# Top-k attention and SoLU layer: in the first batch, one query chunk of each pair of heads per step

## The chip, the cores and the metric

One core of a Trainium2 chip. The metric is the device time of one execution in microseconds. The engines are named as in the profile: PE is TensorE, DVE is VectorE, ACT is ScalarE, POOL is GpSimd, SP is the engine whose queue issues all DMAs here.

## The reference

Attention with eight batches, eight heads, 576 tokens and a head size of 64, in which each query keeps only its 32 largest scores, and behind it a SoLU layer over all 4608 tokens (512 to 1024 to 512).

```python
scores = scale * np.matmul(q, k.transpose(0, 1, 3, 2))
kth = np.partition(scores, -top_k, axis=-1)[..., -top_k:-top_k + 1]
scores = np.where(scores >= kth, scores, -1000000000.0)
attn = np.exp(scores - np.max(scores, axis=-1, keepdims=True))
attn = attn / (np.sum(attn, axis=-1, keepdims=True) + 1e-09)
x = np.matmul(attn, v)          # then (B,H,S,D) -> (B*S, H*D)
...
h = x @ w_in
solu = h * softmax(h)
ln = (solu - mean(solu)) / np.sqrt(var(solu) + 1e-06) * g_ln
out = ln @ w_out
```

## The kernel before

The work is done by `fast_path`; `general_path` stands behind a test at the end, and runs only if a check of the results fails.

**Tiling.** Two heads form a pair (four pairs `hp` in a batch), and the first 512 tokens of a batch form four chunks `t` of 128 queries (every fourth token). The last 64 tokens of the two heads of a pair make one more tile, the tail. A *step* handles four chunks and one tail, that is nine tiles `j` of 128 queries by 576 keys: two heads of each of four chunks and the tail of the pair of chunk 1. A batch takes four steps (0 to 3 for the first), and there are 32. The list `steps` says which pair and which `t` each of the four chunks has. Before the change a step is two pairs with two `t` each: steps 0 and 1 hold `t` = 0 and 1 of all pairs, steps 2 and 3 hold `t` = 2 and 3.

**What one step does.** `load_q` fetches its queries, `prep_q` transposes them on PE. `spread` multiplies them by the moments of the keys, and `spread_v`, `spread_r`, `first_p` and `first` make from this a first guess of the threshold. `scores` computes 128x576 scores into PSUM, `evac` (ACT) copies them to SBUF. `count0`, `count1` and `count2` count the scores above the threshold, on DVE or ACT, and `second`, `third`, `side` move it. `nearest` and `best` take the eight scores nearest to it, `kth` picks the 32nd largest, `exps` (ACT) and `keep` (DVE) make the masked exponentials, `inverse` and `norm` (POOL) divide. `transpose_p` and `transpose_last` turn the result on PE, `copy_p`, `copy_pt` and `copy_last` bring it back (ACT), and `attn_v` multiplies it by the values in two parts of two chunks each. `copy_v` writes the result into `xTm`, which holds two tiles of 128 tokens for all heads.

In `attn_v` and `copy_v`, `runs_of` says whether the two chunks of a part are of one pair. If so, one run of matmuls covers both (256 columns, 320 with the tail); if not, each has its own run (128 columns, or 192 with the tail), with other values.

**Keys.** Before a step may start, the keys of its pairs must be there: `load_k` (with the tails qt and kt), `prep_t`, `prep_k` and `moments` on PE, `prep_tc`, `prep_kc` and `moments_c` on ACT. `load_v` fetches the values.

**SoLU.** A tile of 128 tokens needs all four pairs: `mm1` (two halves), `hexp`, `solu`, `square`, `ln`, `transpose_ln`, `copy_ln`, `mm2` (two halves), `store`. The tails of two batches make one tile. Before the change the tiles 0 and 1 of a batch are complete after its second step.

**Weights.** They arrive as 64-bit floats in 16 chunks, which are turned into 32-bit ones on the way: `load_w`, `w_bits` (DVE), `w_low` (ACT), `w_mul` and `w_add` (POOL), for the second matrix `w_gain`. At the end `w_again`, `w_exp` and `w_check` read them once more and test the exponents.

**What sets the order.** Each piece is entered in a list with a time by `at`; the list is sorted by these times, and each engine gets its instructions in that order. The times order the work and are not waited for. A step's times are `i * STEP` plus an entry of a table: `early_times` has one for each of the first four steps, `step_times` is for all others. `key_times` has one column of times for the first batch and one for all others, `first_times` is for the SoLU tiles of the first batch, `last_times` for those after the last step, `weights_times` for the weights. DMAs of SP are not bound to the written order. What two engines exchange is held by semaphores.

**Buffers.** PSUM has two buffers each for scores, spread and `mm1` (`ps_big`), for transposes (`ps_tp`), and for `attn_v`, `mm2` and the moments (`ps_o`). km has two buffers in SBUF, qt, kt and qm one, kT, mom and the values four. The buffer `e` of the weights' low words is also that of `hexp`.

Of the kernel before, what the change touches and what calls it, by code (L numbers as in the profile page):

```python
# [443 lines left out]
def fast_path(  # L444
# [33 lines left out]
    NP = H // 2  # L478
# [34 lines left out]
    steps = []  # L513
    for b in range(B):
        for t in range(NM):
            two = (t % 2 * 2 + t // 2, t % 2 * 2 + 1 - t // 2)
            steps.append((b, [(hp, t // 2 * 2 + n) for hp in two for n in range(2)]))
# [677 lines left out]
    def at(time, f, *args):  # L1195
        todo.append((time, len(todo), f, args))
# [11 lines left out]
        (scores, range(5), [-7.74, -5.46, -3.54, 0.79, 4.68]),  # L1208
# [28 lines left out]
            (load_q, [()], [-136.1]),  # L1237
            (prep_q, [()], [-49.08]),
            (prep_qc, [()], [-46.09]),
            (spread, [()], [-22.56]),  # L1240
            (spread_v, [()], [-13.82]),
            (spread_r, [()], [-12.57]),
            (first_p, [()], [-11.71]),
            (first, [()], [-3.81]),
            (scores, range(5), [-21.73, -13.84, -9.25, -5.8, 5.01]),
            (evac, range(9), [-18.63, -17.61, -9.77, -3.84, -3.2, -0.35, 5.05, 5.55, 8.61]),
            (count0, range(9), [1.43, -2.43, -1.53, -1.4, 2.24, 3.27, 7.16, 8.56, 8.7]),
            (count1, range(9), [19.93, 27.62, 15.8, 24.5, 16.48, 14.52, 25.06, 25.75, 22.05]),
            (count2, range(9), [45.91, 37.67, 35.49, 32.86, 34.21, 33.88, 48.07, 37.74, 40.71]),
            (second, [()], [10.83]),  # L1250
            (third, [()], [28.34]),
            (exps, range(5), [57.94, 49.7, 61.64, 46.09, 40.28]),
            (side, range(3), [46.05, 39.08, 50.36]),
            (inverse, range(3), [64.9, 68.93, 66.47]),
            (count_off, [()], [59.35]),
            (kth, [()], [60.91]),
            (nearest, range(9), [47.42, 50.7, 47.04, 39.24, 40.26, 39.26, 60.08, 59.88, 52.51]),
            (best, range(9), [48.01, 59.72, 47.48, 39.95, 43.29, 42.83, 60.16, 60.15, 59.98]),
            (keep, range(9), [64.38, 62.62, 62.48, 66.91, 67.31, 68.45, 64.67, 62.84, 61.06]),
            (norm, range(9), [78.27, 66.62, 66.94, 72.53, 69.31, 74.77, 76.06, 70.77, 84.71]),  # L1260
            (transpose_p, range(9), [
                78.29, 66.83, 69.62, 80.13, 73.72, 75.25, 77.68, 81.99, 84.88,
            ]),
            (copy_p, range(8), [84.06, 73.04, 72.36, 85.61, 74.57, 77.94, 84.7, 88.91]),
            (copy_pt, [()], [89.53]),
            (transpose_last, range(2), [85.88, 86.4]),
            (copy_last, range(2), [90.93, 96.41]),
            (attn_v, range(2), [91.57, 101.11]),
            (copy_v, range(2), [101.5, 121.24]),
        ],  # L1270
        [
            (load_q, [()], [-63.22]),
            (prep_q, [()], [-26.27]),
            (prep_qc, [()], [-25.87]),
            (spread, [()], [-22.59]),
            (spread_v, [()], [-21.61]),
            (spread_r, [()], [-20.83]),
            (first_p, [()], [-11.31]),
            (first, [()], [-9.51]),
            (scores, range(5), [-23.24, -22.22, -7.58, -5.59, 4.98]),  # L1280
            (evac, range(9), [-20.42, -15.03, -8.31, -7.32, -2.53, -3.83, 4.56, 6.06, 7.69]),
            (count0, range(9), [1.51, -1.93, -5.39, -3.17, 7.48, 1.22, 4.65, 7.36, 7.75]),
            (count1, range(9), [12.6, 21.87, 22.86, 24.54, 22.25, 19.32, 24.46, 22.34, 14.2]),
            (count2, range(9), [36.07, 31.22, 33.95, 29.01, 30.63, 28.45, 27.23, 37.22, 40.08]),
            (second, [()], [9.1]),
            (third, [()], [25.73]),
            (exps, range(5), [54.75, 52.35, 55.64, 60.46, 56.71]),
            (side, range(3), [41.53, 34.61, 56.64]),
            (inverse, range(3), [63.82, 63.6, 73.38]),
            (count_off, [()], [50.44]),  # L1290
            (kth, [()], [60.1]),
            (nearest, range(9), [42.17, 44.33, 56.1, 41.95, 39.38, 37.61, 59.31, 59.5, 58.57]),
            (best, range(9), [43.9, 46.54, 58.59, 43.63, 40.7, 39.89, 59.58, 59.9, 59.07]),
            (keep, range(9), [63.5, 60.13, 60.62, 63.16, 63.01, 60.7, 67.68, 64.74, 65.7]),
            (norm, range(9), [66.68, 64.54, 68.09, 65.27, 68.2, 66.01, 79.57, 78.32, 75.89]),
            (transpose_p, range(9), [66.85, 70.12, 70.62, 71.87, 76.84, 74.5, 81.76, 80.5, 78]),
            (copy_p, range(8), [70.39, 72.11, 74.48, 76.8, 79.63, 77.7, 82.11, 81.19]),
            (copy_pt, [()], [80.01]),
            (transpose_last, range(2), [86.05, 81.84]),
            (copy_last, range(2), [86.37, 83.08]),  # L1300
            (attn_v, range(2), [86.46, 96.54]),
            (copy_v, range(2), [92.8, 98.93]),
        ],
        [
            (load_q, [()], [-76.41]),
            (prep_q, [()], [-32.91]),
            (prep_qc, [()], [-25.84]),
            (spread, [()], [-18.69]),
            (spread_v, [()], [-11.8]),
            (spread_r, [()], [-11.68]),  # L1310
            (first_p, [()], [-10.43]),
            (first, [()], [-9.45]),
            (scores, range(5), [-22.71, -12.67, -7.53, -2.95, 1.7]),
            (evac, range(9), [-12.31, -12.22, -6.84, -6.24, -4.12, -3.99, -1.57, -0.04, 6.99]),
            (count0, range(9), [-2.44, -0.84, 0.69, 19.56, 4.9, 17.24, 7.58, 2.3, 9.88]),
            (count1, range(9), [23.76, 25.39, 28.42, 21.7, 27.47, 25.78, 27.06, 28.55, 25.68]),
            (count2, range(9), [30.97, 37.36, 39.06, 31.65, 36.22, 33.28, 36.55, 49.83, 41.98]),
            (second, [()], [19.61]),
            (third, [()], [28.64]),
            (exps, range(5), [58.03, 56.1, 60.41, 52.39, 48.63]),  # L1320
            (side, range(3), [46.98, 36.8, 49.89]),
            (inverse, range(3), [66.91, 73.37, 74.37]),
            (count_off, [()], [56.97]),
            (kth, [()], [62.82]),
            (nearest, range(9), [49.3, 59.4, 51.74, 39.5, 41.96, 45.32, 60.81, 60.84, 56.14]),
            (best, range(9), [51.85, 60.58, 59.01, 41.93, 45.25, 46.41, 62.37, 62.67, 59.73]),
            (keep, range(9), [63.28, 63.18, 64.23, 72.39, 65.68, 68.64, 70.02, 73.4, 73.34]),
            (norm, range(9), [67.15, 67.42, 68.98, 73.84, 77.05, 75.85, 74.93, 79.44, 78.1]),
            (transpose_p, range(9), [67.2, 74.04, 79.09, 74.96, 78.87, 77.74, 80.44, 83.19, 83.7]),
            (copy_p, range(8), [73.28, 76.39, 80.9, 77.89, 80.14, 79.48, 84.79, 87.36]),  # L1330
            (copy_pt, [()], [87.38]),
            (transpose_last, range(2), [85.91, 87.61]),
            (copy_last, range(2), [88.63, 90.09]),
            (attn_v, range(2), [90.16, 103.01]),
            (copy_v, range(2), [98.48, 115.16]),
        ],
        [
            (load_q, [()], [-66.4]),
            (prep_q, [()], [-35.36]),
            (prep_qc, [()], [-30.84]),  # L1340
            (spread, [()], [-16.76]),
            (spread_v, [()], [-13.17]),
            (spread_r, [()], [-7.35]),
            (first_p, [()], [-6.37]),
            (first, [()], [-2.89]),
            (scores, range(5), [-14.48, -8.24, -4.39, -2.81, -0.97]),
            (evac, range(9), [-9.51, -8.86, -5.93, -6.05, -1.91, -1.98, -0.4, 0.23, 3.86]),
            (count0, range(9), [-1.72, -1.54, 2.05, 6.45, 5.49, 1.09, 2.45, 8.26, 5.24]),
            (count1, range(9), [11.24, 22.02, 18.49, 13.46, 24.31, 11.77, 18.79, 23.05, 15.93]),
            (count2, range(9), [31.11, 28.29, 30.53, 25.47, 34.71, 38.96, 31.66, 44.39, 26.25]),  # L1350
            (second, [()], [9.95]),
            (third, [()], [24.77]),
            (exps, range(5), [60.62, 50.55, 56.29, 53.12, 56.37]),
# [164 lines left out]
    for b in range(B):  # L1518
        rows = out[b * S : b * S + SM, :].rearrange("(p t) m -> p t m", t=NM)
        n = NP * b + 2  # L1520
# [91 lines left out]
```

## Time and profile before

| | us |
|---|---|
| time, median of 3 runs (1288.27 to 1289.8) | 1289.05 |
| span of the profiled execution | 1288.0 |
| PE busy | 1201.0 |
| DVE busy | 1138.5 |
| ACT busy | 1131.1 |
| POOL busy | 479.7 |

Busy time is that of instructions in execution; the end of a matmul is modelled. In the slices of the page a digit is the busy share of a fortieth of the span (32.2 us) in tenths. Three engines are over 85% busy, so the shares alone don't tell which sets the time: the stretches and the waits must be read. The mean clock that PE was granted over the span is 0.966 of full speed.

### The profile page before, as it was taken

How to read it: one execution, taken by the hardware profiler on the slowest of the kernel's cores; microseconds unless marked ns; L12 is line 12 of the kernel's file. 1: busy time of each engine (PE TensorE's matmuls, PEld its weight loads, DVE VectorE, ACT ScalarE, POOL GpSimd, SP SyncE). 2: the span in 40 equal slices, each digit the busy share in tenths (PEclk: the TensorE clock that was granted, in tenths of full speed). 3: DMA queues.
4: the chain of work that ended last, by engine and by line, in shares of the span. 5: the costliest groups of instructions: out<-in, count | busy, mean ns of one | idle time of the engine just before them, and what ended most of it. 6: DMA issues, size and time to landing. Idle time of an engine off the chain costs nothing.

```text
span 1288.0 us, 20283 instructions
## 1 busy us (share of the span) xinstructions
PE 1201.0 (93%) x6243; PEld 657.0 (51%) x6243; DVE 1138.5 (88%) x2910; ACT 1131.1 (88%) x2478; POOL 479.7 (37%) x583
## 2 busy tenths in 40 slices
PE   6566889999999999999999999999999999998996
PEld 4344444555554555555554555555554555554442
DVE  5899999999998979999999989999999988999512
ACT  4998997999998989999998989999999889998534
POOL 5545523343443223444442224444432334443310
PEclk9577899999999999999999999999999999999998
DMA  8302110011110121011111021011111010102321
GB/s 234 86 27 71 29 38 28 18 39 37 38 37 21 28 55 39 19 31 36 41 35 28 20 62 36 23 30 31 45 37 26 22 38 29 35 9 74 107 74 61
DMA packets 106245, 56.99 MB, mean 44 GB/s; under 512 B 89224, under 2 KB 97424, under 8 KB 106128
## 3 DMA queue, kind: packets, MB, share of 16 engines
q1 hardware_dynamic: 106128, 55.61, 15.5%
q8 instruction: 52, 0.85, 0.3%
q14 instruction: 65, 0.53, 0.1%
HBM read 46.14 MB, written 9.44 MB: 43 GB/s over the span
## 4 chain that ended last, share of the span: by engine, by line
PE 55%; ACT 20%; DVE 17%; issue 4%; POOL 2%; DMA 1%; SPq 0%; DVEq 0%; ACTq 0%; POOLq 0%
PE o_ps L1179 13%; PE s_ps L864 12%; PE h_ps L1121 11%; PE tp_p L1035 7%; PE om L1092 6%; ACT junka L889 4%; DVE junkv L881 4%; DVE E L1006 4%; ACT sg L941 4%; DVE w L969 3%; ACT E L977 3%; DVE w L962 3%; PE tp_ln L1168 2%; ACT PT L1047 2%; ACT X L873 2%
## 5 line engine op out<-in xcount | busy, mean ns | idle before, releaser
L1179 PE MATMUL o_ps<-w_out,lnT 128*128 128x512 f32 x576 | 262.7, 599 | 0.1
L1021 POOL TENSOR_SCALAR E<-E,rden 128x576 f32<-128x576 f32 x256 | 203.7, 811 | 99.3 <-DVE rden L1017 94.2
L881 DVE TENSOR_SCALAR_CACHE_REDUCE junkv<-X,t 128x576 bf16<-128x576 f32 x280 | 224.4, 801 | 15.9 <-ACT X L873 8.3
L934 POOL TENSOR_SCALAR tt<-t 128x9 f32<-128x9 f32 x32 | 20.8, 651 | 560.7 <-DVE t L929 542.7
L1121 PE MATMUL h_ps<-w_in,xTm 128*128 128x512 f32 x512 | 227.5, 595 | 1.1 <-ACT xTm L1107 1.1
L864 PE MATMUL s_ps<-kT,qT 64*128 64x288 f32 x1024 | 201.4, 467 | 15.4 <-ACT qT L780 6.5
L969 DVE MAX8 w<-w 128x8 f32<-128x576 f32 x288 | 210.2, 749 | 0.1
L962 DVE SCALAR_TENSOR_TENSOR w<-X,al,sg 128x576 f32<-128x576 f32 x256 | 210.1, 823 | 0.2
L1006 DVE SCALAR_TENSOR_TENSOR E<-X,kth,E 128x576 f32<-128x576 f32 x256 | 199.0, 815 | 10.2 <-ACT E L977 9.8
L941 ACT ACTIVATE sg<-X,t 128x576 bf16<-128x576 f32 x256 | 196.1, 770 | 0.1
L889 ACT ACTIVATE junka<-X,t 128x576 bf16<-128x576 f32 x232 | 180.3, 777 | 12.7 <-DVE t L912 8.9
L873 ACT ACTIVATE X<-s_ps 128x576 f32<-128x576 f32 x256 | 157.9, 656 | 35.8 <-PE s_ps L864 32.4
L1035 PE MATMUL tp_p<-ident,E 128*128 128x128 f32 x1024 | 155.0, 284 | 15.6 <-POOL E L1021 8.9
L1047 ACT COPY PT<-tp_p 128x512 f32<-128x512 f32 x256 | 147.2, 598 | 22.7 <-PE tp_p L1035 22.5
L1179 PEld LDWEIGHTS o_ps<-w_out,lnT 128*128 128x128 f32 x576 | 104.4, 191 | 109.8 <-issue 107.6
L1035 PEld LDWEIGHTS tp_p<-ident,E 128*128 128x128 f32 x1024 | 116.0, 143 | 85.2 <-issue 42.0
L1121 PEld LDWEIGHTS h_ps<-w_in,xTm 128*128 128x128 f32 x512 | 94.4, 190 | 110.7 <-issue 102.2
L864 PEld LDWEIGHTS s_ps<-kT,qT 64*128 64x128 f32 x1024 | 117.2, 202 | 60.2 <-issue 17.9
L977 ACT ACTIVATE E<-X 128x1152 f32<-128x1152 f32 x128 | 146.6, 1171 | 0.0
L1092 PE MATMUL om<-PT,vm 128*64 128x256 f32 (+1 forms) x1024 | 141.2, 419 | 2.6 <-ACT xTt L1113 2.6
L1092 PEld LDWEIGHTS om<-PT,vm 128*64 128x64 f32 x1024 | 68.9, 139 | 61.9 <-issue 22.2
L829 POOL TENSOR_TENSOR zs<-zs,phalf 128x9 f32<-128x9 f32 x32 | 71.0, 2219 | 2.7
(127 smaller groups left out, 1627.6 us busy)
## 6 DMA issues: line engine op xcount, KB each, us to landing
km<-in_k_dram SPq DMA_DIRECT2D x32, 256.0 KB, 3.3
qm<-in_q_dram SPq DMA_DIRECT2D x128, 64.0 KB, 2.1
vm<-in_v_dram SPq DMA_DIRECT2D x32, 256.0 KB, 2.7
out_dram<-osb SPq DMA_DIRECT2D x32, 256.0 KB, 2.3
w_raw<-in_moe_w_in_dram SPq DMA_DIRECT2D x8, 512.0 KB, 4.9
w_raw<-in_moe_w_out_dram SPq DMA_DIRECT2D x8, 512.0 KB, 3.8
w_again<-in_moe_w_in_dram SPq DMA_DIRECT2D x8, 512.0 KB, 4.4
w_again<-in_moe_w_out_dram SPq DMA_DIRECT2D x8, 512.0 KB, 3.3
```

What stands on the lines that cost most here:

```text
L864: nc.tensor.matmul(out=s[:, half, 0:SH], lhsT=queries_of(i, t)[hd, :], rhs=kT[hd, k0 : k0 + SH], start=True, stop=True,)
L881: nc.vector.tensor_scalar(out=junk, in0=x_of(i, j), scalar1=st[i][t][:, j : j + 1], scalar2=None, op0=ALU.is_ge, op1=ALU.add, accum_out=co ...
L889: nc.scalar.activation(out=junk, in_=x_of(i, j), func=AF.Sign, scale=-1.0, bias=st[i][t][:, j : j + 1], accum_out=columns(i, c)[:, j : j + 1],
L941: nc.scalar.activation(out=d["sg", j], in_=x_of(i, j), func=AF.Sign, scale=-(1.0 + 2.0**-23), bias=d["t2"][:, j : j + 1], accum_out=column ...
L962: nc.vector.scalar_tensor_tensor(out=w, in0=x_of(i, j), scalar=d["al"][:, j : j + 1], in1=d.pop(("sg", j)), op0=ALU.subtract, op1=ALU.mult,)
L969: nc.vector.max(w8[:, j, :], st[i].pop(("w", j)))
L1006: nc.vector.scalar_tensor_tensor(out=e, in0=x_of(i, j), scalar=d["kth"][:, j : j + 1], in1=e, op0=ALU.is_ge, op1=ALU.mult, accum_out=den_a ...
L1021: nc.gpsimd.tensor_scalar(out=e, in0=e, scalar1=st[i]["rden"][:, j : j + 1], scalar2=1.0, op0=ALU.mult, op1=ALU.mult,)
L1035: nc.tensor.transpose(tp[:, c, :], e[:, c * P : (c + 1) * P], ident)
L1092: nc.tensor.matmul(out=o[h * D : (h + 1) * D, cols], lhsT=vm[:, h, c, :] if c < NM else vt[hd, :], rhs=pt[:, h * NM + c, :] if c < NM else ...
L1121: nc.tensor.matmul(out=h[:, half, :], lhsT=x[:, c, :], rhs=w_in[:, c, half * 512 : (half + 1) * 512], start=(c == 0), stop=(c == NP - 1),)
L1179: nc.tensor.matmul(out=o, lhsT=d["lnT"][:, c, :], rhs=w_out[:, c, :], start=(c == 0), stop=(c == NF - 1),)
```

## The change

In the first batch a step is now one `t` of all four pairs. Chunk order within the step turns with `t`, so that chunk 1, whose tail goes with it, is of another pair in each step. A tile of tokens is then complete with one step. All other batches keep their steps. The first batch's SoLU tiles are entered one step earlier (`n` is `NP * b + 1`). The tables `early_times`, `key_times` (both columns), `first_times`, `last_times` and `weights_times` have new numbers; `step_times` differs in one entry, and that of `token_times` and `tails_times` not at all.

```diff
         for t in range(NM):
-            two = (t % 2 * 2 + t // 2, t % 2 * 2 + 1 - t // 2)
-            steps.append((b, [(hp, t // 2 * 2 + n) for hp in two for n in range(2)]))
+            if b == 0:
+                steps.append((b, [(hp % NP, t) for hp in range(t - 1, t + 3)]))
+            else:
+                two = (t % 2 * 2 + t // 2, t % 2 * 2 + 1 - t // 2)
+                steps.append((b, [(hp, t // 2 * 2 + n) for hp in two for n in range(2)]))
...
-        (scores, range(5), [-7.74, -5.46, -3.54, 0.79, 4.68]),
+        (scores, range(5), [-7.74, -5.46, -3.44, 0.79, 4.68]),
...
     key_times = [
-        (load_k, [-186.91, -84.21, -66.88, -51.07], [-71.77, -54.35, -34.54, -26.23]),
-        (load_v, [55.06, 17.62, 49.21, 80.2], [46.71, 33.98, 89.74, 55.28]),
-        (prep_t, [-76.64, -32, -22.27, 26.83], [-50.7, -40.81, -7.18, 29.61]),
-        (prep_tc, [-33.91, -23.58, 2.99, 28.78], [-44.69, -33.63, -1.87, 33.99]),
-        (prep_k, [-55.17, -27.2, -7.7, -0.58], [-57.81, -29.05, -14.02, 12.97]),
-        (prep_kc, [-48.68, -27.05, 2.24, 11.74], [-52.21, -21.98, -13.67, 19.04]),
-        (moments, [-59.71, -45.71, -18.04, -13.23], [-60.64, -32.24, -4.08, 14.96]),
-        (moments_c, [-38.72, -32.17, -15.5, -3.35], [-42.18, -31.04, 2.87, 15.92]),
+        (load_k, [-179.31, -112.44, -96.97, -83.36], [-66.21, -59.83, -42.84, -28.85]),
+        (load_v, [78.62, 52.11, 54.3, 64.51], [35.93, 54.06, 81.63, 87.6]),
+        (prep_t, [-112.7, -85.08, -29.73, -21.59], [-46.07, -31.68, -18.64, 23.63]),
+        (prep_tc, [-55.16, -28.99, -11.74, -20.22], [-29.29, -28.52, -12.43, 28.05]),
+        (prep_k, [-85.5, -39.16, -36.38, -24.68], [-30.7, -26.04, -20.78, 13.78]),
+        (prep_kc, [-56.19, -30.61, -25.14, -22.88], [-27.11, -23.54, -14.85, 18.36]),
+        (moments, [-146.28, -47.56, -28.92, -23.33], [-39.23, -31.8, -19.48, 16.26]),
+        (moments_c, [-38.88, -36.19, -23.61, -20.35], [-32.87, -28.07, 4.31, 19.2]),
     ]
 
     first_times = [
         [
-            (mm1, range(2), [64.27, 63.74]),
-            (hexp, [()], [67.94]),
...
+            (mm1, range(2), [86.16, 90.45]),
+            (hexp, [()], [100.33]),
...
     last_times = [
...
-        (copy_ln, range(2), [95.04, 105.72]),
-        (mm2, range(2), [106.44, 112.11]),
-        (store, [()], [204.61]),
...
+        (copy_ln, range(2), [96.25, 103.85]),
+        (mm2, range(2), [105.86, 111.22]),
+        (store, [()], [169.21]),
     ]
...
-        n = NP * b + 2
+        n = NP * b + (2 if b else 1)
```

Left out are the new numbers of `early_times`, of the other tiles of `first_times`, of the rest of `last_times` and of `weights_times`.

## The prediction

> **What bounds the kernel now.** I read the page's forty slices first, then busy time by stretch, then the waits inside the early stretches.
>
> ```profile
> PE   6566889999999999999999999999999999998996
> ...
> DVE  5899999999998979999999989999999988999512
> ACT  4998997999998989999998989999999889998534
> ...
> PEclk9577899999999999999999999999999999999998
> ```
>
> TensorE is full from about slice 8 to the end; before that VectorE and ScalarE are full and TensorE is not, at a clock of 0.5 to 0.9. In the last slices TensorE alone is full. So the end is set by TensorE: its 1201.0 us of work plus what it idles, and its idling lies at the start.
>
> ```profile
> core 0: us, PE busy (x) PEld busy (x) DVE busy (x) ACT busy (x) POOL busy (x), PEclk, DMA share, GB/s
> 40.00:112.00 72.00, 47.36 (x227) 26.44 (x221) 69.43 (x171) 68.81 (x152) 33.34 (x36) 0.62 0.15 37
> 112.00:146.00 34.00, 26.82 (x152) 14.73 (x149) 30.19 (x66) 32.79 (x77) 17.62 (x15) 0.91 0.20 58
> 146.00:190.00 44.00, 36.03 (x197) 20.14 (x197) 40.59 (x106) 40.32 (x92) 21.45 (x26) 0.88 0.16 38
> 190.00:234.00 44.00, 42.16 (x194) 21.49 (x192) 41.21 (x106) 35.29 (x78) 16.58 (x20) 0.96 0.11 32
> 234.00:1140.00 906.00, 895.98 (x4837) 494.39 (x4838) 854.11 (x2214) 845.54 (x1850) 327.33 (x403) 1.00 0.13 33
> ```
>
> Columns: stretch, its length, busy us of each engine, clock. From 40 to 112 VectorE and ScalarE limit together (3 us idle each), from 112 to 146 ScalarE (1.2 us idle). From 234, where the scores of step 6 begin, TensorE idles 10 us in 906. A microsecond gained or lost before 234 therefore comes through to the end.
>
> **What the Trainium skill says.** "TensorE: Matmul & The Clock Gate", What's actually happening: the array runs at half rate until it has been busy for about 3.4 us. The trace agrees: after a wait of 3.26 us at 188.77, eight matmuls of L1179 take 4.33 us in the chain of waits, later ones 3.43. "DMA: Bandwidth & Descriptors", Anatomy of one DMA: about 2 us fixed before a transfer counts as landed; here a 32 KB qt lands 2.1 to 5.4 us after issue, median 2.9. "Perfetto Trace Analysis", Optimizing Scalar/DVE Operations: every instruction has a fixed access cost, so larger operations are better. The trace agrees: a 128x256 copy takes 364 ns (L1107), a 128x128 one 289 (L712).
>
> **The change, part by part.**
>
> *Start.* Step 0 now needs the keys of four pairs, not two. On the SP queue five weight chunks stand ahead of the fourth key load, as now. The tails qt and kt have one buffer, so each pair's load waits for the previous pair's transposes:
>
> ```profile
> 14.21 0.61 SPq L670 DMA_DIRECT2D km<-in_k_dram  x1
> 18.05 0.60 SPq L676 DMA_DIRECT2D qt<-in_q_dram  x1
> ```
> ```profile
> 17.66 0.36 PE L706 MATMUL pre<-ident,qt 64*128 64x64 f32 x1 [3.05 <-DMA qt<-in_q_dram]
> 17.91 0.37 PE L706 MATMUL pre<-ident,kt 64*128 64x64 f32 x1
> 18.02 2.29 PE L864 MATMUL s_ps<-kT,qT 64*128 64x288 f32 x8
> ```
>
> The fourth qt and kt are issued at 18.05 and 18.76; with 2.9 us they land near 21.7. Then come prep_t 3, the spread matmuls (1.1 us) and the scores, at about 23.2 instead of 18.0: +5.2. Chunks now follow each other every 3.0 to 3.7 us (18.0, 21.05, 24.2, 27.9, 31.6). The key transposes between them go, so I take 2.9: the tail's scores begin at 34.8 (35.9 if prep_q 1's 1.1 us doesn't hide), take 1.8 and are evacuated by 37.5. Its two ScalarE counts (0.88 each) end at 39.3. `second 0` stands at 35.16 now: **+4.1 us**. Weight preparation moves into the wait, so not all of VectorE's time is lost (bounds 0 to +6).
>
> *Around 106 to 117.* ScalarE now waits 1.99, 0.28 and 0.76 us for scores of step 3, held by `spread_v 3`, behind seven `keep`. After the change it stands behind four (0.74 each), and `inverse 1.0` behind three. ScalarE, which is late, has these 3.0 us to catch up in: **-3.0** (bounds -3.5 to 0).
>
> *Split runs.* Each attn_v part of batch 0 now has two runs: eight parts go from 10 to 20 matmuls, eight copy_v from one 128x256 to two 128x128. Sixteen matmuls of 320 columns take 2.37 us, of 256 columns 1.95: per pair 296 and 244 ns, so a fixed part of 36 ns. Five more pairs in each of eight parts: 1.4 us, half of it after 150, where TensorE limits: **+0.7** (upper bound for all eight 5 us, if each short matmul costs a 110 ns transpose). Each copy costs 2 x 289 - 364 = 214 ns; four lie where ScalarE limits: **+0.8**. The others lie beside TensorE.
>
> *Tile 0 and what follows it.* A tile is whole after its own step, but in the new order mm1 of tile 0 stands only some eight pieces earlier, and tile 3 no earlier: the SoLU work is not brought a whole step forward. What moves is what stood in its way:
>
> ```profile
> 141.98 1.28 POOL L640 TENSOR_TENSOR w_low<-w_low,w_tmp 128x512 f32<-128x512 f32 x1 [3.24 <-ACT w_low L616]
> 146.49 0.69 POOL L934 TENSOR_SCALAR tt<-t 128x9 f32<-128x9 f32 x1 [3.23 <-DVE t L929]
> 147.15 1.83 POOL L643 TENSOR_TENSOR w_out<-w_tmp,w_low 128x512 f32<-128x512 f32 x1
> ```
>
> The last weight's addition (L643) stood behind step 3's `tt`; hexp of tile 0 shares its buffer and began at 149.0, solu at 150.8, and solu's end let the scores of step 4 go on (152.14). Now the last count1 of step 3 comes before three exps (3 x 1.06), prep_qc 4 (0.47) and two copies (0.8), 4.4 us of ScalarE work earlier: 145.7 - 4.4 + (4.1 - 3.0 + 0.8) = 143.2. After it VectorE has two `best` (1.33), `kth` (1.9), three `keep` (2.2), `inverse` (0.4), `spread_v 4` (0.95): solu at 150.0 with its small steps, against 150.8, and the scores 1 us earlier: **-2.9** against the sum of the parts so far (+1.9). Bounds: -4.4, or nothing.
>
> *Step 5.* Now TensorE stands still ahead of the transposes of step 3:
>
> ```profile
> 188.77 1.09 PE L1035 MATMUL tp_p<-ident,E 128*128 128x128 f32 x8 [3.26 <-POOL E L1021]
> 189.79 2.19 PE L864 MATMUL s_ps<-kT,qT 64*128 64x288 f32 x8
> 191.91 4.40 PE L1179 MATMUL o_ps<-w_out,lnT 128*128 128x512 f32 x8
> ```
>
> In the new order mm2 of tile 0 (its first half) and the scores of chunk 5.0 stand ahead of these transposes: 4.3 + 2.1 us of work into the wait. That takes the 3.26 and 0.9 for the slow clock: **-4.2** (bounds -5, or -1 if VectorE's `keep` of step 3, with `spread_v 5` now among them, comes 3 us later).
>
> *Later batches.* prep_t, prep_k and moments stand elsewhere in all seven; the instructions are the same, so I take **0**. Without a row for the new order: -3 (a third of the 10 us idle) to +8.
>
> *End.* TensorE works through from 1196 to 1275 but for 1 us. The last tiles' halves change places; behind the last output copy stand three w_check instead of two (0.85), and the last but two store stands earlier (-0.25): **+0.6** (0 to +1).
>
> The new load order on SP lets four w_again stand ahead of fewer stores; stores have 10 us of slack here. POOL's order of norms costs nothing where TensorE limits.
>
> Sum: 4.1 - 3.0 + 0.8 - 2.9 - 4.2 + 0.7 + 0.6 = -3.9 us on the span of 1288.0, which was taken with a run of 1289.83; the median run is 1289.05. So 1285.
>
> **The rivals.**
> - *A, the sum above*, 1285, own range 1281 to 1288.
> - *B, the start's delay is not made good*: with ScalarE 95% and VectorE 96% busy from 40 to 112, +4.1 stays and only the wait at 188.77 pays for it: 1289 + 4.1 + 0.8 - 4.2 + 0.7 + 0.6 - 2.9 is 1288. Against it: 3.0 us of waits are there to be used. That the tile's early completion doesn't bring SoLU forward speaks for it.
> - *C, slower: key preparation in the seven later batches.* prep_k 12 now stands between the two transpose_last of step 9, so the second waits for copy_last, behind an evacuation (0.6), a count2 (0.77) and itself (0.3); attn_v of the same step then waits for prep_tc, whose PSUM buffer it takes. I work out 1.15 us a batch against 0 to 0.75 now: at most 8 us in seven batches, 1285 + 8 = 1293. It decides from 0.95 us a batch. Against it: ScalarE has 60 us idle in those 906.
> - *D, more than the sum*: mm1 of tile 0 also fills half of the 7.2 us that TensorE idles from 112 to 146 (3.6), and the later batches idle 3 us less: 1278. Against it: ScalarE limits there.
>
> **How the numbers follow.** A 0.47, B 0.21, C 0.24, D 0.08. About 0.2%, 2.6 us, is what this measurement can tell from no change. Faster by more: A 0.40, D 0.08, B 0.04: 0.52. Within: A 0.07, B 0.12, C 0.02: 0.21. Slower: C 0.22, B 0.05: 0.27. The range, from D's side to past C: 1278 to 1294.
>
> **What would show it.** Right: first scores at 22 to 24, `second 0` near 39, scores of step 4 by 152, no wait over 1.5 us before step 3's transposes, scores of step 6 at 228 to 232, and from there to the end the same length within 2 us. Wrong: scores of step 4 after 155 (B), or a stretch from step 6 to the end over 4 us longer, with waits before L1069 and L1092 for ScalarE (C).

## The result, and the profile after

The changed kernel is slower: 1296.45 us, median of four runs (1293.07 to 1297.62), against 1288.66 for the kernel before (four runs); ratio 1.0055, 95% interval 1.0035 to 1.0075. A second series of six runs gave 1295.27, ratio 1.0049 (1.0036 to 1.0061). So the change costs 6 to 8 us. The prediction said 1285, with a range to 1294; it had the wrong sign.

The profiled execution of the changed kernel has a span of 1294.5 us against 1288.0, +6.5. Line numbers of the changed kernel are 3 above those of before from L514 on. First the slices of its page (engine, then a digit for each fortieth of the span):

```profile
PE   5757789999999999999999999999999999998995
...
DVE  4799999999999888999999888999999888999511
ACT  3889998999998989999999989999999889998533
...
PEclk9997899999999999999999999999999999999998
```

VectorE and ScalarE are a digit lower in the first slice, and most of the rest looks as before: nothing here says where 6 us went. Stretches that begin and end with the same piece of work do. Both tables are cut at `third` of steps 0, 2, 3 and 4, at `first` of step 6, and near the end; columns are the stretch, its length, the busy us (and count) of PE, PEld, DVE, ACT and POOL, the granted clock, DMA share and GB/s. The kernel before:

```profile
0.00:46.60 46.60, 27.75 (x141) 17.01 (x141) 28.87 (x61) 27.18 (x67) 27.67 (x41) 0.89 0.71 206
46.60:108.60 62.00, 40.52 (x196) 22.66 (x196) 60.06 (x153) 59.26 (x129) 24.98 (x28) 0.64 0.12 31
108.60:146.20 37.60, 30.36 (x163) 16.64 (x162) 33.73 (x72) 36.03 (x85) 20.82 (x19) 0.87 0.21 59
146.20:180.90 34.70, 29.99 (x153) 16.95 (x152) 31.77 (x79) 31.02 (x69) 19.05 (x22) 0.85 0.14 35
180.90:236.60 55.70, 50.60 (x255) 26.44 (x254) 52.12 (x136) 46.99 (x105) 21.39 (x26) 0.97 0.14 38
236.60:1140.20 903.60, 893.58 (x4821) 492.76 (x4820) 852.05 (x2209) 843.14 (x1844) 324.92 (x400) 1.00 0.13 33
```

The changed kernel:

```profile
0.00:52.50 52.50, 33.22 (x145) 19.55 (x145) 27.90 (x59) 28.01 (x66) 26.96 (x40) 1.00 0.65 185
52.50:114.80 62.30, 35.04 (x176) 21.09 (x177) 60.46 (x147) 57.41 (x125) 25.12 (x24) 0.96 0.09 23
114.80:154.70 39.90, 33.58 (x206) 20.17 (x203) 36.51 (x70) 35.15 (x86) 24.32 (x22) 0.84 0.24 64
154.70:190.90 36.20, 31.08 (x222) 20.13 (x223) 34.82 (x90) 34.73 (x76) 17.13 (x21) 0.87 0.08 18
190.90:243.00 52.10, 50.73 (x319) 29.37 (x318) 50.68 (x136) 46.77 (x107) 23.27 (x27) 1.00 0.16 41
243.00:1146.00 903.00, 888.73 (x4817) 492.46 (x4816) 850.83 (x2209) 842.98 (x1847) 326.29 (x400) 1.00 0.13 33
```

The clock column needs care. The clock records of a trace begin late, at 32.9 us in this trace of the kernel before and at 92.2 in that of the changed one, and the views (the page's row of slices and the mean clock as well) count the time ahead of the first record as full speed. The score matmuls tell the rate there too: one lasts 681 to 847 ns where half rate is recorded, 402 to 507 where full rate is, and 681 to 846 ahead of the first record. So both kernels start at half rate, and the 0.89 in the first row of the kernel before and the 1.00 and 0.96 in the first two of the changed one are too high. Counted with that, the second row holds about 45 us of half rate in both kernels: the clock does not make a difference there.

Read by length: +5.9 up to `third` of step 0, +0.3, +2.3, +1.5, then -3.6, and -0.6 over the seven later batches; about +0.7 comes at the end. The loss is made in the first 52 us and nothing after it wins it back: what step 5 gains (-3.6) the stretches ahead of it have lost (+4.1).

*The start.* From TensorE's early work in the changed kernel (start, duration, operation, in brackets the wait before it):

```profile
18.41 0.37 PE L709 MATMUL pre<-ident,qt 64*128 64x64 f32 x1
...
21.52 1.09 PE L722 MATMUL tp_qk<-ident,km 128*128 128x128 f32 x4 [2.29 <-DMA km<-in_k_dram]
...
22.89 0.37 PE L709 MATMUL pre<-ident,qt 64*128 64x64 f32 x1
...
24.19 12.55 PE L867 MATMUL s_ps<-kT,qT 64*128 64x288 f32 x32
36.67 1.12 PE L722 MATMUL tp_qk<-ident,qm 128*128 128x128 f32 x4
37.72 2.18 PE L867 MATMUL s_ps<-kT 64*64 64x288 f32 x8
```

TensorE waits until 21.52 for km of the fourth pair to come; that pair's qt is transposed at 22.89, the first scores follow at 24.19 (18.02 before), and the tail's at 37.72 (31.55 before). `second` of step 0, from the list of VectorE's instructions, waits for the tail's count:

```profile
42.28 0.16 DVE L910 SCALAR_TENSOR_TENSOR step<-c,tb 128x2 f32<-128x2 f32 x1 [2.50 <-ACT junka L892]
```

It stood at 35.16 before: +7.1 us.

*Steps 2 and 3.* These are the waits that TensorE's scores have for `spread_v`:

```profile
82.16 6.59 PE L867 MATMUL s_ps<-kT,qT 64*128 64x288 f32 x16 [1.91 <-DVE mean L815]
...
113.78 2.28 PE L867 MATMUL s_ps<-kT,qT 64*128 64x288 f32 x6 [5.34 <-DVE mean L815]
```

And ScalarE's for the scores of step 2:

```profile
84.83 0.65 ACT L876 ACTIVATE X<-s_ps 128x576 f32<-128x576 f32 x1 [1.43 <-PE s_ps L867]
...
88.80 1.19 ACT L876 ACTIVATE X<-s_ps 128x576 f32<-128x576 f32 x2 [1.62 <-PE s_ps L867]
```

ScalarE no longer waits 3.0 us for the scores of step 3, but now it waits 3.3 us (with a third wait of 0.29) for those of step 2, where the kernel before has 0.3: there `spread_v` 2 came behind `third` 1 with only an `inverse` between, now two `keep` stand there.

*From `third` 2 to `third` 3*, the stretch that is 2.3 us longer, ScalarE idles 4.75 us (1.57 before), and 4.1 of it are waits for TensorE. The two longest:

```profile
130.89 0.58 ACT L1050 COPY PT<-tp_p 128x512 f32<-128x512 f32 x1 [1.30 <-PE tp_p L1038]
...
133.05 0.65 ACT L876 ACTIVATE X<-s_ps 128x576 f32<-128x576 f32 x1 [1.57 <-PE s_ps L867]
```

By the clock records TensorE runs at half rate for 12.6 us of this stretch (0.84 in the table). The run after_bufs (below) has the same order of work there, and its stretch reads:

```profile
113.10:150.70 37.60, 29.92 (x206) 18.25 (x203) 36.43 (x70) 34.95 (x86) 24.30 (x22) 0.95 0.24 68
```

Half rate lasts 3.4 us in it, ScalarE waits 0.7 us for TensorE, and the stretch is as long as in the kernel before (37.6). The seven traces of the changed kernel and its variants part in the same way: 39.3 to 39.9 us in the four with some 12 us of half rate, 37.6 to 38.1 in the three with 3.4 to 3.5. So these 2.3 us go with the clock of the single execution, and not with the order of work alone. (The kernel before has 9.7 us of half rate in its stretch and loses nothing by it, so the new order seems the more sensitive one.) Why the rate fell in some executions and not in others is not shown.

*Tile 0.* POOL's lines that answer to those shown of before:

```profile
151.75 1.28 POOL L643 TENSOR_TENSOR w_low<-w_low,w_tmp 128x512 f32<-128x512 f32 x1 [4.71 <-ACT w_low L619]
...
154.95 0.21 POOL L937 TENSOR_SCALAR tt<-t 128x9 f32<-128x9 f32 x1 [1.93 <-DVE t L932]
155.12 1.27 POOL L646 TENSOR_TENSOR w_out<-w_tmp,w_low 128x512 f32<-128x512 f32 x1
```

`tt` of step 3 comes at 154.95 (146.49 before), the weight's addition ends at 156.4, hexp of tile 0 starts at 158.5 and solu at 161.3 (150.8 before, +10.5). The scores of step 4 begin at 163.85.

*Step 5.* TensorE now goes on where it stood still for 3.26 us:

```profile
193.55 3.70 PE L1182 MATMUL o_ps<-w_out,lnT 128*128 128x512 f32 x8
198.12 1.09 PE L1095 MATMUL om<-PT,vm 128*64 128x128 f32 x16 [0.87 <-ACT kT L716]
```

The first half of mm2 takes 3.70 us here (4.40 before), and is followed by a wait of 0.87.

### The profile page after: what moved, and what is told of

Same layout as the page of the kernel before. It is cut to its first block, busy times and chain, and to the rows that moved or that the text cites. A ratio compares the mean times of both kernels' runs of the same rounds, so it can differ in the third digit from the quotient of the medians.

```text
span 1294.5 us, 20607 instructions
## 1 busy us (share of the span) xinstructions
PE 1200.9 (93%) x6403; PEld 667.4 (52%) x6403; DVE 1140.4 (88%) x2910; ACT 1133.0 (88%) x2486; POOL 484.0 (37%) x583
## 3 DMA queue, kind: packets, MB, share of 16 engines
q1 hardware_dynamic: 106128, 55.61, 15.6%
## 4 chain that ended last, share of the span: by engine, by line
PE 54%; ACT 24%; DVE 15%; issue 4%; POOL 2%; DMA 1%; SPq 0%; DVEq 0%; ACTq 0%
PE o_ps L1182 13%; PE s_ps L867 12%; PE h_ps L1124 10%; PE om L1095 7%; PE tp_p L1038 7%; ACT junka L892 5%; ACT sg L944 4%; DVE E L1009 4%; DVE junkv L884 4%; ACT E L980 3%; ACT PT L1050 3%; PE tp_ln L1171 2%; DVE w L972 2%; DVE w L965 2%; ACT X L876 2%
## 5 line engine op out<-in xcount | busy, mean ns | idle before, releaser
L965 DVE SCALAR_TENSOR_TENSOR w<-X,al,sg 128x576 f32<-128x576 f32 x256 | 213.1, 835 | 0.1
L892 ACT ACTIVATE junka<-X,t 128x576 bf16<-128x576 f32 x232 | 180.4, 778 | 13.8 <-DVE t L915 9.6
L1038 PE MATMUL tp_p<-ident,E 128*128 128x128 f32 x1024 | 151.5, 281 | 8.2 <-POOL E L1024 3.8
L1095 PE MATMUL om<-PT,vm 128*64 128x320 f32 (+3 forms) x1152 | 144.2, 395 | 0.9 <-ACT kT L716 0.9
L1095 PEld LDWEIGHTS om<-PT,vm 128*64 128x64 f32 x1152 | 77.0, 142 | 59.2 <-issue 21.8
```

What stands on the lines that cost most here:

```text
L892: nc.scalar.activation(out=junk, in_=x_of(i, j), func=AF.Sign, scale=-1.0, bias=st[i][t][:, j : j + 1], accum_out=columns(i, c)[:, j : j + 1],
L965: nc.vector.scalar_tensor_tensor(out=w, in0=x_of(i, j), scalar=d["al"][:, j : j + 1], in1=d.pop(("sg", j)), op0=ALU.subtract, op1=ALU.mult,)
L1038: nc.tensor.transpose(tp[:, c, :], e[:, c * P : (c + 1) * P], ident)
L1095: nc.tensor.matmul(out=o[h * D : (h + 1) * D, cols], lhsT=vm[:, h, c, :] if c < NM else vt[hd, :], rhs=pt[:, h * NM + c, :] if c < NM else ...
```

## The experiments

Three theories stood at the outset. T1: the loss is the later start, and a shift of the start passes to the end. T2: the order of the work in steps 1 to 4 costs it, whatever the start. T3: the split runs of `attn_v` cost it.

The table gives, for each run's profiled execution, how much later than in the kernel before a few marks come (us, from the starts of the instructions: `third` of steps 0, 3 and 4, `first` of step 6, the last matmul), and then the medians of its timed runs. Runs whose names begin with before_ start from the kernel before, those with after_ from the changed one. The ratio is not formed from the two medians, so the last columns can differ: for after_bufs 4.5 us by the medians, 0.46% or 5.9 us by the ratio. From the last matmul to the end of the span it is 9.1 us in the kernel before and 7.6 to 10.5 in others that end in the same code, and up to `third` 0 identical code differs by up to 1.2 us, so single executions carry that much.

| run | third 0 | third 3 | third 4 | first 6 | last matmul | median against before | ratio (95%) |
|---|---|---|---|---|---|---|---|
| changed kernel | +5.9 | +8.5 | +10.0 | +6.4 | +6.4 | +7.8 | 1.0055 (1.0035 to 1.0075) |
| changed kernel, again | +5.0 | +6.9 | +9.1 | +5.6 | +5.9 | +6.2 | 1.0049 (1.0036 to 1.0061) |
| after_bufs | +4.2 | +4.5 | +6.0 | +2.5 | +2.3 | +4.5 | 1.0046 (1.0029 to 1.0063) |
| after_keys1st | +10.7 | +11.1 | +12.7 | +9.2 | +10.0 | +10.6 | 1.0086 (1.0072 to 1.0101) |
| after_order | +3.4 | +5.3 | +7.6 | +4.0 | +4.2 | +3.5 | 1.0029 (1.0017 to 1.0040) |
| after_spread2 | +3.3 | +5.2 | +7.4 | +3.9 | +3.9 | +3.0 | 1.0024 (1.0010 to 1.0038) |
| after_act | +3.2 | +4.0 | +8.5 | +5.0 | +5.2 | +6.1 | 1.0052 (1.0039 to 1.0064) |
| before_late | +1.8 | +2.7 | +1.2 | +1.1 | +1.6 | +1.7 | 1.0013 (1.0005 to 1.0021) |
| before_start | -2.0 | -2.1 | -1.6 | -1.7 | -1.8 | -1.3 | 0.9994 (0.9986 to 1.0002) |
| before_spread3 | -0.4 | +1.1 | +0.9 | +2.2 | +2.0 | +1.4 | 1.0010 (1.0002 to 1.0018) |
| before_step5 | -0.9 | -0.4 | -1.9 | +0.3 | +0.1 | +1.2 | 1.0014 (1.0008 to 1.0021) |
| before_step5b | +0.7 | +0.6 | +0.5 | -2.1 | -2.4 | -1.1 | 0.9991 (0.9985 to 0.9998) |
| before_split0 | -1.2 | -0.6 | -0.8 | +0.9 | +0.6 | +0.8 | 1.0005 (0.9998 to 1.0011) |
| before_split | +0.4 | +0.6 | +0.6 | +1.1 | +14.8 | +13.8 | 1.0101 (1.0087 to 1.0116) |
| before_best | -2.0 | -1.3 | -2.8 | -5.4 | -4.5 | -2.0 | 0.9983 (0.9976 to 0.9990) |

### A buffer for each tail

```diff
-            d[nm + "t"] = p1.tile([ST, 2, D], F32, tag=nm + "t", name=nm + "t")
+            pool, tag = (p9, "sg") if n < NP else (p1, nm + "t")
+            d[nm + "t"] = pool.tile([ST, 2, D], F32, tag=tag, name=nm + "t")
```

> The changed kernel, in which the tails qt and kt of the first batch's four pairs get a buffer each (in the nine buffers of sg, idle until then), so that their loads no longer wait for the previous pair's transposes. T1 (the loss is the later start, and it passes through to the end): the loads of pairs 2 and 3 follow at once, the first scores begin about 3.5 us earlier (20 to 21 instead of 24.2), and the whole time falls by 3 to 4 us, to about 1293. T2 (the loss is the order of the work in steps 1 to 4, between 90 and 170 us, which would absorb an earlier start): the first scores come as early, the time falls by less than 1 us. T3 (the loss is the split runs of attn_v): no more than 1 us.

Measured 1293.41, median of six (1291.2 to 1297.59). By the medians that is 1.9 us less than the second series of the changed kernel, by the ratios (1.0046 and 1.0049) 0.4: no difference that these runs can tell. Its profiled run is the fastest of the six, and TensorE ran at full rate for most of its stretch from `third` 2 to `third` 3, so its row in the table flatters it. The first scores came at 23.07, only 1.1 us earlier than 24.19: TensorE waited for other things (1.68 for a copy of ScalarE, behind w_low) where it had waited for tails. So the tails' single buffer was one link of several, and T1's full 3 to 4 us was not there to be had in this way.

### The keys ahead of the weights

```diff
-        (load_k, [-179.31, -112.44, -96.97, -83.36], ...
+        (load_k, [-379.31, -372.44, -366.97, -363.36], ...
```

with km of the first batch in the buffers of `vm`, and the tails as above.

> As the run with a buffer for each tail, and the key loads of all four pairs stand ahead of all weight chunks on SP's queue (km in the buffers of vm too). The weights come some 8 us later, and with them the first w_low on ScalarE, which stands ahead of the keys' copies. T1: first scores at 17 to 20 us, the time falls by 4 to 7 us against the changed kernel. T2 and T3: less than 1 us. If the later weights hold VectorE and ScalarE instead (w_bits ahead of spread_v), the first scores come no earlier than 22, and the time falls by less than 3 us under T1 too.

Measured 1299.53, the worst of all. The case written last had happened, and more: the first w_low on ScalarE waited for its weights until 14.34, the second until 19.12, the keys' copies stood behind both, and the first scores came at 29.55. It failed as a mend, but it is the largest shift in the table: +10.7 at `third` 0 and +10.0 at the last matmul.

### The first scores of the kernel before, later and earlier

Later: the matmuls of chunk 0 four times over.

```diff
-        for half in range(2):
+        for half in [0, 1] * (4 if (i, t) == (0, 0) else 1):
```

> The kernel before, in which the eight matmuls of the first scores (chunk 0 of step 0) are done four times over, with the same result. At the slow clock each repetition takes about 2.3 us, so `second 0` comes some 5 to 7 us later; nothing else is moved. T1: the delay passes to the end, +4.5 to +7 us. T2, T3, and my prediction's catch-up of 3 us: the kernel has slack there, and no more than +3 us comes through.

TensorE in this run:

```profile
17.59 7.09 PE L864 MATMUL s_ps<-kT,qT 64*128 64x288 f32 x32
25.42 1.78 PE L864 MATMUL s_ps<-kT,qT 64*128 64x288 f32 x8 [0.49 <-ACT X L873]
27.47 1.77 PE L864 MATMUL s_ps<-kT,qT 64*128 64x288 f32 x8
29.76 2.09 PE L864 MATMUL s_ps<-kT,qT 64*128 64x288 f32 x8
32.36 1.19 PE L864 MATMUL s_ps<-kT 64*64 64x288 f32 x8
```

The size of the delay was misjudged. The repetition takes 4.8 us longer (7.09 against 2.29), but the next three chunks take 1.78, 1.77 and 2.09 instead of 2.83, 2.74 and 2.71, and the tail's scores begin only 0.8 us later than before. What is left at `third` 0 is +1.8, and it reaches the end: +1.6 at the last matmul, +1.7 in the medians. By the expected numbers this would be T2's case (no more than +3). But the delay that arrives at `third` 0 is itself only 1.8 us, and that passes nearly whole.

Earlier: prep_t of pair 2 behind the scores of chunk 0.

```diff
-        (prep_t, [-76.64, -32, -22.27, 26.83], ...
+        (prep_t, [-76.64, -32, -21.6, 26.83], ...
```

> The kernel before, with the two tail transposes of pair 2 (prep_t 2) behind the first scores on TensorE's queue instead of ahead of them: the first scores no longer wait for the tails of a pair that they don't use (3.05 us in the trace). T1 (what the start gains or loses passes to the end one to one): the first scores begin near 15 instead of 18.0, third of step 0 comes 1.5 to 3 us earlier, and so does the end: -1.5 to -3. T2 (between step 1 and step 5 there is slack that takes up a shift): within 0.7 us of before.

```profile
14.46 1.32 PE L864 MATMUL s_ps<-kT,qT 64*128 64x288 f32 x2
16.87 1.77 PE L864 MATMUL s_ps<-kT,qT 64*128 64x288 f32 x5 [1.09 <-DVE mean L812]
```

The scores begin at 14.46 and not at 18.02, `third` 0 is 2.0 us earlier, the last matmul 1.8, the median 1.3 (0.8 by the ratio, whose interval just includes no change). This speaks for T1 in the other direction too, without settling it.

### The order of step 0's scores in the changed kernel

On top of after_bufs. In step 0 chunk 0 is of pair 3, whose keys land last, and the changed kernel scores it first. Here chunk 1 and the tail (pair 0) go first, then chunk 2, the spread, chunks 3 and 0; evacuations, counts and the copies of prep_tc 2 follow.

```diff
-            (scores, range(5), [-18.11, -13.57, -12.89, -8.45, 3.12]),
+            (scores, range(5), [-12.89, -38.5, -26, -18.11, -37.5]),
```

> The changed kernel with a buffer for each tail, in which step 0 no longer begins its scores with chunk 0, which is of pair 3 whose keys land last: chunk 1 and the tail (pair 0) come first, ahead of the key transposes of pairs 2 and 3, then chunk 2 (pair 1), the spread, chunk 3 (pair 2) and chunk 0 (pair 3); evacuations and counts follow the same order. T1: first scores near 15, second of step 0 at 36 to 38 instead of 42.3, and the whole 4 to 6 us below the changed kernel: near 1291. T2 (the order of steps 1 to 4 costs it whatever the start): 1294 to 1296.

First scores at 15.60, `second` of step 0 at 38.77 (42.28), `third` 0 at +3.4, median 1292.28: 3.0 us below the second series of the changed kernel, 4.2 below the first. Near T1's number, and outside T2's. The two changes together are clear of the scatter (seven runs from 1289.35 to 1294.64, ten of the changed kernel from 1292.55 to 1297.62); what each is worth is not.

Over the first six rows, which are the changed kernel twice, its three variants with another start, and after_spread2 below, the shift at the last matmul less that at `third` 0 is +0.5, +0.9, -1.9, -0.7, +0.8 and +0.6. So in these traces the end is late by about what the start is late. The rest of the change, its losses up to `third` 4 and its gain in step 5, cancels out; the -1.9 is after_bufs, whose stretch up to `third` 3 had the faster clock.

### Split runs

In all batches, and in the first alone:

```diff
-        if chunks[n][0] == chunks[n + 1][0]:
+        if False:
```
```diff
-        if chunks[n][0] == chunks[n + 1][0]:
+        if steps[i][0] > 0 and chunks[n][0] == chunks[n + 1][0]:
```

> The kernel before, in which every attn_v and copy_v of all batches is done in two runs (128 columns, and 128 or 192), also where both chunks are of one pair: the cost of split runs, magnified, 64 parts instead of the 8 that the change splits. T3, at my prediction's price of 36 ns a pair of matmuls and 0.2 us a copy: +11.5 us on TensorE and more where the copies hold it, +12 to +20. T1: the trace of the changed kernel shows no more TensorE time for its split parts, so 0 to +3 us.

> The kernel before, in which attn_v and copy_v are done in two runs in the first batch alone, as the changed kernel has it, with everything else as before. From the run with all batches split (+13.8 us for 64 parts) 8 parts come to +1.7 us; my prediction's own sum was +1.5 (0.7 on TensorE, 0.8 on ScalarE). If the early batch hides it: 0. If split runs are what costs the changed kernel its time between 108 and 190 us (T3): +3 or more.

Splitting all 64 parts costs 13.8 us. The page's row of TensorE:

```profile
PE 1216.6 (93%) x7523; PEld 717.3 (55%) x7523; DVE 1139.0 (87%) x2910; ACT 1138.0 (87%) x2542; POOL 477.7 (37%) x583
```

Against 1201.0 us and 6243 matmuls that is 15.6 us for 1280 more, 12 ns each. T3's mechanism is real. My price came near it through two errors that offset each other: a cut adds 20 matmul records to a part, as the counts show, where I priced 10, and a record costs 12 ns where I took 18 (36 a pair). But only eight parts are split by the change, and those cost 0.8 us (the interval reaches from -0.3 to +1.4). T3 is not what makes the changed kernel slow.

### The catch-up of step 3, alone

In the table of step 3:

```diff
-            (spread_v, [()], [-13.17]),
+            (spread_v, [()], [-14.95]),
```

> The kernel before, in which only spread_v of step 3 moves on VectorE, from behind seven keep to behind four, as in the new kernel. My prediction's term for this was -3.0 us (ScalarE catches up at 106 to 117). The trace of the new kernel speaks for another reading: there the waits are gone but the same time was spent before, as VectorE's work only changed places; then the three keep, with norm and transposes behind them, come 1.06 us later and nothing is gained, -0.5 to +1.

Instead of gaining 3.0 us it loses 1.4. ScalarE's waits at that place:

```profile
109.03 0.78 ACT L941 ACTIVATE sg<-X,t 128x576 bf16<-128x576 f32 x1 [2.24 <-DVE t L929]
111.47 0.59 ACT L1047 COPY PT<-tp_p 128x512 f32<-128x512 f32 x1 [1.57 <-PE tp_p L1035]
113.70 1.19 ACT L873 ACTIVATE X<-s_ps 128x576 f32<-128x576 f32 x2 [0.88 <-PE s_ps L864]
```

The 3.0 us for the first scores of step 3 are gone; 2.24 us for `third` 2, 1.57 for transposes that hang on the delayed `keep`, and 0.88 have come, 4.7 in all. The same instructions wait, for other neighbours on VectorE. after_spread2 tried the mirror of it in the changed kernel: `spread_v` 2 back to right behind `third` 1, on top of after_order; in the table of step 2:

```diff
-            (spread_v, [()], [-13.71]),
+            (spread_v, [()], [-14.05]),
```

> The changed kernel with a buffer for each tail and the scores of step 0 in the order of the pairs (1292.3 us), in which only spread_v of step 2 goes back, on VectorE, from behind two keep to right behind third of step 1, where the kernel before has it. In the changed kernel's trace the scores of step 2 wait 1.91 us for it, and ScalarE 3.4 us for these scores. If this is where the catch-up of step 3 was paid: 1.5 to 2 us less than that run, about 1290.5. If VectorE is simply full there (what one spread_v gains, two keep lose): within 0.7 us of it.

0.7 us less in the medians (1291.58), 0.1 at `third` 3 in the trace: no difference that these runs can tell. The scores began 0.8 us earlier (78.83) and then waited 0.75 us for ScalarE's evacuation.

### The wait at 188.77, alone

First with the scores of chunk 5.0 and then mm2 ahead of step 3's transposes:

```diff
-            (transpose_p, range(9), [69.88, 69.41, ...
+            (transpose_p, range(9), [70.95, 70.8, ...
```

> The kernel before, in which only the order around the wait at 188.77 is changed as the new kernel has it: the scores of chunk 5.0 and the first half of mm2 of tile 0 stand ahead of the first two transposes of step 3. My prediction's term for this was -4.2 us, on a path that TensorE sets: expected -3.3 to -4.2. If what follows was waiting for ScalarE or VectorE anyway (T2), less than 1 us.

```profile
186.34 0.72 PE L864 MATMUL s_ps<-kT,qT 64*128 64x288 f32 x2 [3.20 <-DVE rs L1137]
187.65 2.28 PE L864 MATMUL s_ps<-kT,qT 64*128 64x288 f32 x6 [0.58 <-DVE solu L1140]
```

The wait of 3.26 for POOL became one of 3.78 for solu of tile 1, whose PSUM buffer the scores take, and the kernel 1.2 us slower. What is brought forward has to be ready. The second try put mm2 of tile 0 first (the transposes stay moved as above), and gave it its buffer in time:

```diff
-            (mm2, range(2), [109.64, 111.75]),
+            (mm2, range(2), [108.9, 111.75]),
...
-        at(n // NP * NP * STEP + (later if n >= NP else first)[n % NP], f, n)
+        at(n // NP * NP * STEP + (later if n >= NP else first)[n % NP] - ({prep_t: 6.4, prep_tc: 10.7}.get(f, 0.0) if n == 7 else 0.0), f, n)
```

> The kernel before, with the order around the wait at 188.77 changed so that what is brought forward doesn't itself wait: the first half of mm2 of tile 0, then the scores of chunk 5.0, then the first two transposes of step 3; and, since mm2 takes the PSUM buffer of pair 7's tail transposes, these and their two copies on ScalarE are brought forward too (prep_t 7, prep_tc 7). In the earlier run without this, the scores waited 3.78 us for solu of tile 1 in place of the wait removed. If the term of my prediction is real (-4.2 us for this place, of which 3.26 is the wait): -2.5 to -4. If TensorE's wait there is only the sign of late VectorE and ScalarE work (T2): within 1 us of before.

```profile
185.78 3.70 PE L1179 MATMUL o_ps<-w_out,lnT 128*128 128x512 f32 x8
189.41 1.84 PE L864 MATMUL s_ps<-kT,qT 64*128 64x288 f32 x8
191.19 1.09 PE L1035 MATMUL tp_p<-ident,E 128*128 128x128 f32 x8
```

No wait, and 2.6 us gained between `third` 4 and `first` 6 in this execution. The median is 1.1 us lower (interval 0.3 to 1.9): the sign is settled, the size lies between these two.

### Tile 0 in the changed kernel

On top of after_order, the copies that TensorE waits for at 150 to 161, and hexp and solu of tile 0, go ahead of w_low, exps and `keep`:

```diff
-            (hexp, [()], [100.33]),
-            (solu, [()], [104.94]),
+            (hexp, [()], [95.7]),
+            (solu, [()], [102.5]),
...
-            (copy_last, range(2), [85.27, 100.84]),
+            (copy_last, range(2), [85.27, 95.65]),
```

and prep_kc 5 by 1.16, prep_qc 4 by 3.28 earlier.

> The changed kernel with a buffer for each tail and step 0's scores in the order of the pairs (1292.3 us), in which ScalarE serves TensorE first between 147 and 161 us: the copies of prep_kc 5, prep_qc 4 and copy_last of step 1 and the hexp of tile 0 stand ahead of w_low and of two exps of step 2, and solu of tile 0 ahead of the keep of step 2 on VectorE. In the trace TensorE waits there 2.4, 2.0 and 0.7 us for these copies, and solu ends 8 us after its place in the kernel before. If the term of tile 0 (-2.9 in my prediction, +1.5 to +2.3 in the traces) failed through this order alone: 2 to 3.5 us less than that run, near 1289.5. If ScalarE and VectorE are simply behind there and whatever goes first makes another wait: within 0.8 us of it.

It is slower: 1295.18, 2.9 us above after_order. solu of tile 0 came 4.8 us earlier (+2.6 instead of +7.4 against before), and the scores of step 4 with it:

```profile
154.76 0.75 PE L868 MATMUL s_ps<-kT,qT 64*128 64x288 f32 x2 [1.79 <-DVE solu L1144]
158.56 2.25 PE L868 MATMUL s_ps<-kT,qT 64*128 64x288 f32 x6 [3.05 <-DVE mean L816]
```

Their second half then waits 3.05 us for `spread_v` 4, which VectorE reaches later. That is nearer to the second expected case (another wait is made), but worse than its 0.8 us. Beside it ran the changed kernel itself, for more runs:

> The changed kernel itself, unaltered, beside the runs before it on the same chip: its median has so far four runs from 1293.1 to 1297.6. Expected 1295 to 1297; then the buffers for the tails are worth 2 to 3 us and the order of step 0's scores 1 to 2 more. At 1294 or less, the buffers would be worth nothing that can be told.

1295.27, as expected. By the medians the buffers for the tails are worth 1.9 us and the order of step 0's scores 1.1 more; by the ratios 0.4 and 2.2. Only the 3 us of both together are shown.

### Both findings in the kernel before

The edits of before_start and before_step5b together.

> The kernel before with the two changes that the runs so far point to: the first scores ahead of pair 2's tail transposes (alone -1.3 us) and the new order around the wait at 188.77 (as in the run beside this one). If a shift of the start passes through and the wait is a separate term, the two add up: 1.3 us more than the run beside it alone, in all -4 to -5 us, about 1284.5. If not, no faster than the better of the two.

1286.55 us, median of 21 (1284.31 to 1287.83): 2.0 us less than the kernel before, ratio 0.9983 (0.9976 to 0.9990). The two add up (1.3 and 1.1 alone, 2.0 together), though to half the expected sum at most. It is faster than both kernels, clear of the noise.

## Why the prediction was wrong

By its own steps:

- **Start, +4.1: too small.** It measured +7.1 at `second` 0. The mechanism was right, the size came from two choices. The fourth tail was used at 22.89 instead of 21.7 (first scores 24.19 for 23.2, +1.0): I priced its own landing, but km of the same pair came at 21.5, and its transposes and moments stand ahead. And I took 2.9 us for a chunk and let prep_q 1 hide, so that the tail's scores would begin 11.6 us after the first; they begin 13.5 us after (12.55 for four chunks, 3.1 each, and 1.1 for prep_q 1 that doesn't hide), +1.9. The bound of +6 was passed as well.
- **Catch-up at 106 to 117, -3.0: it does not exist.** This is the step that failed in kind. I counted a wait that the new order removes and not what the same order puts in its place: 3.3 us of the same wait in step 2 (from `third` 0 to `third` 2 the kernel is 0.3 us longer, not 3.0 shorter), and in before_spread3, where it is moved alone, +1.4 us. VectorE is 97% busy there; putting `spread_v` ahead of `keep` only changes who waits.
- **Tile 0 and what follows, -2.9: it did not come either.** ScalarE's last count1 of step 3 was to come at 143.2 and came at 154.1. Three exps and prep_qc 4 do stand behind it now, as said; but it started 6.2 us late (`third` 2) and not 1.1, and ScalarE idled 4.75 us in that stretch against 1.57. The stretch from `third` 3 to `third` 4 is 1.5 us longer instead of 2.9 shorter. after_act gave tile 0 its earlier place by hand, and lost. The 4.75 us are for the most part waits for TensorE at half rate, as shown above; in after_bufs ScalarE idles 2.65 us there.
- **Step 5, -4.2: right in kind, a little large.** From `third` 4 to `first` 6 the changed kernel and all its variants gain 3.5 to 3.6 us; alone it is worth 1.1 to 2.6, and it costs 1.2 when what is brought forward is not ready (before_step5).
- **Split runs, +1.5: right in size, by luck.** +0.8 measured in the first batch alone (the interval includes 0), +1.7 scaled from all batches; the count was half of what it is and the price per matmul half too high.
- **Later batches, 0: right**, -0.6 in 903 us. Rival C, which had most of the chance for slower, is refuted: the key preparation in its new places costs nothing. **End, +0.6: right**, +0.7.

Rival B came nearest: it had the start's delay passing to the end, and even the reason (ScalarE 95%, VectorE 96% busy). It reached 1288 and not 1296 mostly because it kept the small start, the tile's -2.9 and the whole of -4.2. Without the two gains that failed and with the measured start, my own sum would read 5.9 + 1.5 - 4.2 + 0.6 = +3.8. Of the 2.6 us that are left to +6.4, nearly all lie between `third` 0 and `third` 4, and the 2.3 that go with TensorE's half rate in this execution are of that size. The run after_bufs, without them, fits the same sum: 4.2 + 1.5 - 4.2 + 0.6 = +2.1, and its last matmul came +2.3. Two single executions don't prove a sum to the microsecond. The signs to look for had been named rightly: the scores of step 4 came at 163.85, after 155, which was to speak for B, and the stretch from step 6 to the end kept its length.

## What to carry to other kernels

Where two engines are full, an instruction moved forward on one of them removes a wait and makes another of its size behind it; count such a gain only when the work that it passes has slack of its own, and look for the same move in the neighbouring steps, where it may go the other way. A delay before the full engines start was not made good later here: price the first results chunk by chunk, with each buffer's turn-round, and ask which operand of the first piece lands last. Something brought forward into a wait fills it only if its own inputs and buffers are free by then. Read a clock column together with the length of the same instruction in stretches whose rate is known, and compare several executions before a stretch's length is put down to the order of work.

## What the runs showed of the hardware

Extra matmuls were almost free at the start. 24 more of them took 4.8 us, and the next three chunks became 2.6 us faster (5.6 us of matmuls instead of 8.3). In that trace (before_late) a score matmul goes from 684 ns to 403 at 23.5 us, 5.9 us after the repetition began, and the first clock record, of full rate, begins at 23.6. The Trainium skill says in "TensorE: Matmul & The Clock Gate", What's actually happening, that the array runs at half rate until it has been kept busy. This trace agrees. A row of matmuls without a recorded pause was not enough, though: in the changed kernel 32 score matmuls take 12.55 us, 392 ns from one to the next, and each still lasts 681 to 846 ns. What keeps the rate down there was not tried, nor was other work for TensorE ahead of the first scores.

VectorE's operations with two inputs took longer where POOL was busy. `nearest` takes 874 ns on average where it overlaps an instruction of POOL in the changed kernel (105 of 288), and 808 where it doesn't (848 and 808 before); `best`, with one input, takes 752 and 748 in both kernels, within 1 ns. "GPSIMD Engine Reference", Specifications, says that POOL shares its way to SBUF with VectorE and that instructions with two SBUF inputs contend; the trace agrees. Between `third` 0 and `third` 4 VectorE's busy time grew from 125.6 to 131.8 us: 2.7 us are one more chunk of weights in `w_bits`, and 3.0 us the 36 `nearest`, as many as before. Whether this costs time by itself was not tested.
